# A planner's exp costs, the first block's PSUM halves, and when the last block's Q is made, in a fused attention and MLP block

## The chip, the cores and the metric

One core of a Trainium2 chip runs the kernel. The metric is device time in microseconds (us) of one execution. Before the change it is 780.84 us (median of 3 runs, 779.88 to 781.1). The engines are PE (TensorE: matmuls), DVE (VectorE), ACT (ScalarE), POOL (GpSimd) and SP (SyncE, which issues nearly all DMAs). Each works through its own queue in order and waits on semaphores for the others.

## The reference

One transformer block on 2048 tokens of 512 features, with 32 heads of 16 columns. Shift, scale and gate of both halves come from a conditioning row `c`.

```python
mod = (silu(c) @ w_mod)               # sa, ca, ga, sb, cb, gb: six rows of 512
h = layernorm(x) * (1 + ca) + sa
q, k, v = split_heads(h @ wqkv)       # 32 heads x 16
p = softmax(q @ k.T * 16 ** -0.5)
x = x + ga * ((p @ v) @ wo)
h = layernorm(x) * (1 + cb) + sb
x = x + gb * (gelu(h @ w1 + b1) @ w2 + b2)     # 512 -> 1376 -> 512
```

## The kernel before

**Blocks and runs.** The tokens are cut into four blocks of 512; a partition holds four tokens of a block (t = 0 to 3). For each block the kernel norms and transposes the tokens, projects K, V and Q, and then goes through its *runs*. A run is one block of queries against all 2048 keys for four heads, which lie side by side in the four row groups of 32 partitions. One key tile (128 keys) of a run gives four *scores*, matrices of 128 by 512, one a head. The first three blocks have 24 runs (block, group of 128 columns `cc`, parity of the head). The last block is cut differently: a run takes half of the queries for both parities (runs 24 to 29), and its last 256 queries go in quarters of 128 (runs 30 to 33; `tile_of` says which tokens: t = 2 for runs 30 and 31, t = 3 for 32 and 33). In all there are 2048 scores; run 24 begins at score 1536.

**Two ways to exponentiate.** Most scores are computed by PE into one of two PSUM tensors, `st3` (three banks) and `st2` (two), in turn, and exponentiated by ACT in one instruction of three or two scores (`qk_a`, L1022). The rest go one at a time into an `ax` bank, where DVE makes 16-bit integers `ph` of them whose bits are read as bf16 (L1063); four more integer additions on the whole tile (L1079 on DVE for three of them, and for the fourth either pieces on POOL, L1101, or what is left on DVE, L1095) and five sets of scaled values `VX` average the error of that approximation. `next_tile` gives key tiles to ACT or to DVE as either runs dry. Weighted sums of V, and of ones for the denominators, gather in the bank `od` (`pv_op`, L1162).

**Normalising.** When a run ends, `normalise` copies `od` (L1201), sends the denominators through DRAM to spread them over partitions (DMAs L1207, L1209, reciprocal on DVE L1212, DMAs L1217 and four of L1222), multiplies on POOL (L1228) and shifts rows into place (four DMAs, L1189). For the last runs `quick` does it on DVE alone: transpose, reciprocal, transpose, multiply (L1450 to L1456).

**The order.** Nothing above runs in the order it is written. `Plan` is a list scheduler in Python: every operation has an engine, a cost in us, the operations it depends on, and a priority; the planner starts what can start first, breaks near ties by priority plus a pseudo-random `spread` (one entry of `SEEDS` for each 12.5 us), and emits the instructions in that order. `A_US` is its cost of an exp of one, two or three scores. `later` holds back PE work that is not due yet: it starts only when PE has been less than full lately (`fill_at`). A `chain` is a group of matmuls into one `ax` bank, cut into pieces that the planner may put other work between. There are two `ax` banks.

**Q.** `want_q(g)` asks for the query projections up to group g. For the last block, groups 12 to 15 serve runs 24 to 27 first (and 28 to 33 again). A Q is four matmuls (L833), one DVE copy (`qs`, L869) and eight DMAs of 16 rows on SP's queue (`qm<-qs`, L875). `qk_deps` asks when the scores of a run are made; `due` tells when the matmuls stop being held back.

**The first norm.** `first_norm` is the way to the first exp: DVE makes statistics (L681, L682), POOL the power -1/2 (L692), DVE the normed tokens z (L698), PE the modulation columns (L675, from four loads of `w_mod`) and the transposes (L811), and DVE and ACT apply the modulation (L706, L703). *Part* 0 is tokens t = 0 and 1, part 1 is t = 2 and 3; j = 0 to 3 are the four column groups of 128. In the kernel before, DVE's j (0 and 1) lie in one PSUM tensor and ACT's (2 and 3) in the other, both parts of it in different banks. In the built program the transposes of part 1 into a tensor wait for the engine that reads part 0 out of it.

Of the kernel before, what the change touches and what calls it, by code (L numbers as in the profile page):

```python
# [12 lines left out]
ALU = mybir.AluOpType  # L13
# [50 lines left out]
SEEDS = (105, 215, 995, 503, 989, 957, 458, 92, 83, 614, 508, 48, 986, 458, 1, 279, 770, 174, 798, 975, 118, 230, 617, 767, 151, 936, 102, 752, 533, 869, 305, 310, 674, 762, 539, 481, 234, 244, 942, 69, 6, 273, 821, 447, 288, 502, 920, 725, 621, 485, 469, 573, 221, 692, 877, 666, 310, 622, 566, 733, 603, 368, 946, 826)  # L64
# [222 lines left out]
def kernel(  # L287
# [37 lines left out]
    COLD, EARLY = 4.4, 4.6  # L325
    SPAN = (3, 2)
    POOL_US, POOL_MIN = 0.68, 0.5
    A_US = {1: 0.49, 2: 0.9165, 3: 1.3435}
# [50 lines left out]
    def prog():  # L379
        return units[0] / 2  # L380
# [37 lines left out]
    def later(o):  # L418
        return o.kind not in ("qkA", "qkD", "pv", "last", "part", "heat") and o.kind not in urgent and o.due > prog()
# [135 lines left out]
    for h in range(2):  # L555
        o_x0 += 2 * [dma(lambda o, h=h: nc.sync.dma_start(out=o_x[0].tile[:, 2 * h:2 * h + 2, :],
                                                         in_=x_src[0][:, 2 * h:2 * h + 2, :]),
                         (o_x[0],), kb=210, prio=0.2 * h - 5.0)]
# [10 lines left out]
    def load_mod(j):  # L569
        def go(o):  # L570
            first[j] = nc.sync.dma_start(out=mod_cols(j), in_=wm_src[:, j, 0:2 * D])
        return dma(go, (o_mod,), kb=250, prio=0.2 * j - 4.6)
# [205 lines left out]
    def first_norm(kind):  # L778
# [10 lines left out]
        def scale(t):  # L789
# [5 lines left out]
              for t in range(TPB)]  # L795
# [3 lines left out]
                0.17, [mm] + o_plus, lat=0.03, prio=0.0, rel=(mm,))  # L799
# [3 lines left out]
        for part in range(2):  # L803
            for half, e in enumerate(("DVE", "ACT")):
                def view(half=half, part=part):
                    return banks[half].tile.bitcast(BF16)[:, 2 * part * QB:2 * part * QB + QB]

                def tr(o, half=half, part=part, view=view):
                    for j in range(2):
                        for t in range(2):  # L810
                            nc.tensor.transpose(out=view()[:, (2 * j + t) * P:(2 * j + t + 1) * P],  # L811
                                                in_=z.tile[:, 2 * part + t, (2 * half + j) * P:(2 * half + j + 1) * P],
                                                identity=ident)
                trs.append(op("PE", tr, 4 * 0.0575, za[2 * part:2 * part + 2] + [banks[half], o_id], lat=PEL,
                              mode=("full", 0), kind=kind, rel=(z,), prio=0.0))
                for n in range(2):
                    j = 2 * half + n
# [892 lines left out]
```

## Time and profile before

| | us |
|---|---|
| median of 3 runs (range) | 780.84 (779.88 to 781.1) |
| the profiled execution | 780.36 |
| its span (first to last instruction) | 778.5 |
| begin to first exp on ACT | 14.56 |
| first exp to end of the last | 745.2 |
| behind the last exp | 18.7 |

The span is what the profile covers; 1.86 us of the profiled execution lie around it. The granted TensorE clock is full throughout. The page of the profile gives each engine's busy time and the costliest groups of instructions; a row of the timeline is start, length, engine, line, operation and tile, and in brackets the idle time of the engine before it and what ended that.

### The profile page before, as it was taken

The page shows a single profiled execution, that of the slowest core. Times are in us where ns is not written, and L with a number is a line of the kernel's source. Part 1 is how long each engine was busy: PE and PEld are TensorE (multiplying, and loading weights), DVE is VectorE, ACT ScalarE, POOL GpSimd, SP SyncE. Part 2 cuts the span into 40 slices and gives each one's busy share as a digit, 9 for nine tenths or more (in the row PEclk, how much of TensorE's full clock was granted, in tenths as well). Part 3 has the DMA queues.
Part 4 walks back from the last instruction along what each step waited for, and adds up shares of the span by engine and source line. Part 5 has one row for each costly group of instructions (what it writes and reads, how often), then busy time and mean ns, then how long its engine had stood idle before and what let it go on. Part 6 is the DMA issues. An engine that isn't in the chain of part 4 may idle for free.

```text
span 778.5 us, 22044 instructions
## 1 busy us (share of the span) xinstructions
PE 726.3 (93%) x8886; PEld 274.8 (35%) x8964; DVE 725.6 (93%) x1294; ACT 751.3 (97%) x671; POOL 242.1 (31%) x466
## 2 busy tenths in 40 slices
PE   8899989999999999999999999999989999999998
PEld 3433333233332232232322232222334443444565
DVE  6889979999999999999999999998989999989984
ACT  4999999999999999999999999999989999999995
POOL 6522433512454532233324123322121222410310
PEclk9999999999999999999999999999999999999999
DMA  7152001100021101000100000001110001001000
GB/s 217 38 164 64 19 16 43 27 23 12 11 77 22 29 18 51 17 23 10 39 19 23 29 17 19 24 18 32 30 56 22 18 19 37 26 16 32 27 6 29
DMA packets 35248, 27.65 MB, mean 36 GB/s; under 512 B 18029, under 2 KB 29010, under 8 KB 35146
## 3 DMA queue, kind: packets, MB, share of 16 engines
q1 hardware_dynamic: 35138, 26.24, 12.1%
q8 instruction: 70, 1.15, 0.7%
q14 instruction: 32, 0.26, 0.1%
q10 hardware_dynamic: 8, 0.00, 0.0%
HBM read 20.64 MB, written 2.60 MB: 30 GB/s over the span
## 4 chain that ended last, share of the span: by engine, by line
ACT 36%; PE 27%; DVE 22%; issue 11%; DMA 2%; POOL 1%; SPq 0%; DVEq 0%; POOLq 0%; ACTq 0%
ACT pt L1022 35%; DVE ph L1063 10%; PE od L1162 8%; PE st L974 7%; DVE sh L1079 6%; PE ax L1335 3%; PE ax L974 2%; PE ax L1400 2%; DVE ln_s L681 2%; PE ax L833 1%; DMA dc<-dn 1%; DVE sh L1095 1%; DVE OD L1201 1%; PE ax L1329 1%; ACT g L1417 1%
## 5 line engine op out<-in xcount | busy, mean ns | idle before, releaser
L1022 ACT ACTIVATE pt<-st 128x1536 bf16<-128x1536 f32 x626 | 711.6, 1317 | 6.9 <-PE ax L974 3.7
L1063 DVE TENSOR_SCALAR ph<-ax 128x512 int16<-128x512 f32 x484 | 317.2, 683 | 20.0 <-PE ax L974 18.0
L974 PE MATMUL st<-qm,kT 32*128 32x512 bf16 (+1 forms) x1664 | 246.1, 370 | 21.0 <-ACT pt L1022 15.7
L1079 DVE TENSOR_SCALAR sh<-ph 128x2048 int16<-128x2048 int16 x363 | 242.5, 699 | 2.0 <-PE od L1162 1.2
L1101 POOL TENSOR_TENSOR sh<-ph,pair_sh 128x256 int32<-128x256 int32 x198 | 119.4, 611 | 286.5 <-DVE sh L1079 184.6
L974 PE MATMUL ax<-qm,kT 32*128 32x512 bf16 (+1 forms) x512 | 169.8, 367 | 9.5 <-DVE ph L1063 5.8
L1162 PE MATMUL od<-sh,VX 128*32 128x512 bf16 (+2 forms) x2640 | 171.5, 327 | 2.7 <-DVE sh L1079 2.0
L974 PEld LDWEIGHTS <-kT 32*128 32x128 bf16 x2176 | 81.1, 91 | 237.6 <-issue 225.1
L1162 PE MATMUL od<-pt,VEB 128*32 128x512 bf16 (+2 forms) x2156 | 141.6, 324 | 0.8 <-ACT pt L1022 0.3
L1162 PEld LDWEIGHTS <-VX 128*32 128x32 bf16 x2640 | 61.1, 95 | 84.0 <-issue 73.2
L1162 PEld LDWEIGHTS <-VEB 128*32 128x32 bf16 x2816 | 65.4, 96 | 70.3 <-issue 56.1
L1095 DVE TENSOR_SCALAR sh<-ph 128x2048 int16<-128x2048 int16 (+3 forms) x95 | 52.8, 563 | 0.3
L1228 POOL TENSOR_TENSOR OT<-OD,RB 128x256 bf16<-128x256 f32 x37 | 27.2, 745 | 75.2 <-DVE sh L1079 58.1
L1162 PE MATMUL od<-ph,VEB 128*32 128x512 bf16 (+2 forms) x660 | 48.2, 326 | 0.7 <-DVE OD L1201 0.7
L1400 PE MATMUL ax<-blk,W 128*128 128x512 bf16 (+1 forms) x153 | 40.5, 352 | 1.3 <-issue 0.6
L901 POOL TENSOR_SCALAR VX<-VEB 128x128 bf16<-128x128 bf16 x64 | 25.2, 394 | 38.7 <-DVE VEB L713 35.5
L1335 PE MATMUL ax<-w,g 128*128 128x512 bf16 x110 | 30.9, 381 | 1.8 <-DVE ph L1063 1.1
L833 PE MATMUL ax<-blk,w 128*128 128x512 bf16 x92 | 29.9, 382 | 2.0 <-issue 0.9
L1228 POOL TENSOR_TENSOR OS<-OD,RB 128x256 bf16<-128x256 f32 x24 | 17.3, 728 | 42.0 <-DVE sh L1079 23.6
L1407 DVE TENSOR_SCALAR g<-ax,b1c 128x512 bf16<-128x512 f32 x33 | 24.5, 744 | 0.2
L1335 PEld LDWEIGHTS <-g 128*128 128x128 bf16 x187 | 15.4, 97 | 23.1 <-issue 11.9
L681 DVE BATCH_NORM_STATS2 ln_s<-xb 128x6 f32<-128x512 bf16 x31 | 21.1, 680 | 1.4 <-DMA xb<-in_A_x_dram 1.4
(125 smaller groups left out, 408.3 us busy)
## 6 DMA issues: line engine op xcount, KB each, us to landing
RB<-rn SPq DMA_DIRECT2D x120, 64.0 KB
xb<-in_A_x_dram SPq DMA_DIRECT2D x7, 512.0 KB
qm<-qs SPq DMA_DIRECT2D x120, 16.0 KB
out_dram<-o SPq DMA_DIRECT2D x15, 128.0 KB
W<-in_B_w_dram SPq DMA_DIRECT2D x1, 1376.0 KB
w<-in_A_wqkv_dram SPq DMA_DIRECT2D x3, 384.0 KB
g<-in_w_mod_dram SPq DMA_DIRECT2D x4, 256.0 KB
xb<-in_w_mod_dram SPq DMA_DIRECT2D x2, 512.0 KB
```

What stands on the lines that cost most here:

```text
L681: nc.vector.bn_stats(out=st6, in_=src)
L833: return chain([(lambda ps, j=j: nc.tensor.matmul(out=ps[:, 0:QB], lhsT=w.tile[:, j, cc * P:(cc + 1) * P], rhs=o_h[b].tile[:, j, :], start ...
L974: nc.tensor.matmul(out=o.tile[:, k * QB + n * w:k * QB + (n + 1) * w], lhsT=kT[cc][kb][rows, ko * P:(ko + 1) * P], rhs=qm.tile[rows, par, ...
L1022: nc.scalar.activation(out=e.tile[:, 0:len(got) * QB], in_=o.tile[:, 0:len(got) * QB], func=ACT.Exp, scale=ESC)
L1063: nc.vector.tensor_scalar(out=ph.tile[:, o.row * QB:(o.row + 1) * QB], in0=o.tile, scalar1=PH_B, scalar2=0.0, op0=ALU.add, op1=ALU.max)
L1079: sh = op("DVE", lambda o, j=j: nc.vector.tensor_scalar(out=o.tile, in0=first.tile, scalar1=PH_SH[j], scalar2=None, op0=ALU.add), 0.6, es, ...
L1095: return nc.vector.tensor_scalar(out=sh.tile[:, at], in0=first.tile[:, at], scalar1=PH_SH[-1], scalar2=None, op0=ALU.add)
L1101: return nc.gpsimd.tensor_tensor(out=sh.tile[:, at].bitcast(I32), in0=first.tile[:, at].bitcast(I32), in1=pair_sh[:, 0:1].to_broadcast([P, ...
L1162: nc.tensor.matmul(out=o_od[r].tile[32 * i:32 * i + 32, to:to + w], lhsT=v_tile(k, ph)[:, c0:c0 + 32], rhs=got[i][:, n * w:(n + 1) * w], s ...
L1228: two = beside(lambda c: nc.gpsimd.tensor_tensor(out=both_heads(OT.tile, tile_of[r]) if r in tile_of else OT.tile[:, c], in0=OD.tile[:, c] ...
L1335: nc.tensor.matmul(out=ps, lhsT=g[:, f, col:col + P], rhs=rhs[:, c], start=(f == 0), stop=(f == NF - 1))
L1400: mm = chain([(lambda ps, f=f, j=j, f0=f0: nc.tensor.matmul(out=ps[:, (f - f0) * N:(f - f0 + 1) * N], lhsT=W1[:, j, f * P:(f + 1) * P], rh ...
```

## The change

- **Costs of exps**: `A_US` is 0.012 us smaller for one score and 0.011 for two and three; `COLD` and two costs of loads (`kb`) and of the first modulation change too, all in the planner's accounts alone. All 64 `SEEDS` are new (not shown).
- **Pieces of a chain that has begun** are not held back by `later` any more.
- **The first norm**: the two PSUM tensors now hold part 0 and part 1, each with all four j in one bank, so DVE and ACT both read both; PE transposes a part in one operation of eight. The modulation columns get a lower priority than the z of the last tokens.
- **Q of the last block**: group r - 8 is asked for by run r, and its due time is one run earlier for groups 13 to 15.
- **Run 30** is normalised by `quick` too, and POOL's multiplications of the last six runs are not held back until DVE leaves room.

```diff
-    COLD, EARLY = 4.4, 4.6
+    COLD, EARLY = 4.6, 4.6
-    A_US = {1: 0.49, 2: 0.9165, 3: 1.3435}
+    A_US = {1: 0.478, 2: 0.9055, 3: 1.3325}
...
     def later(o):
-        return o.kind not in ("qkA", "qkD", "pv", "last", "part", "heat") and o.kind not in urgent and o.due > prog()
+        return not o.cont and o.kind not in ("qkA", "qkD", "pv", "last", "part", "heat") and o.kind not in urgent and o.due > prog()
...
-                         (o_x[0],), kb=210, prio=0.2 * h - 5.0)]
+                         (o_x[0],), kb=210 if h else 315, prio=0.2 * h - 5.0)]
...
-        return dma(go, (o_mod,), kb=250, prio=0.2 * j - 4.6)
+        return dma(go, (o_mod,), kb=200 if j else 450, prio=0.2 * j - 4.6)
...
         mA = op("DVE", lambda o: nc.vector.tensor_tensor(out=modA, in0=mm.tile[:, 0:2 * NC], in1=plus, op=ALU.add),
-                0.17, [mm] + o_plus, lat=0.03, prio=0.0, rel=(mm,))
+                0.17, [mm] + o_plus, lat=0.03, prio=0.51, rel=(mm,))
...
         for part in range(2):
-            for half, e in enumerate(("DVE", "ACT")):
-                def view(half=half, part=part):
-                    return banks[half].tile.bitcast(BF16)[:, 2 * part * QB:2 * part * QB + QB]
...
+            def view(j, part=part):
+                return banks[part].tile.bitcast(BF16)[:, j * HB:(j + 1) * HB]
+
+            def tr(o, part=part, view=view):
+                for j in range(NC):
+                    for t in range(2):
+                        nc.tensor.transpose(out=view(j)[:, t * P:(t + 1) * P],
+                                            in_=z.tile[:, 2 * part + t, j * P:(j + 1) * P], identity=ident)
+            trs.append(op("PE", tr, 8 * 0.0575, za[2 * part:2 * part + 2] + [banks[part], o_id], lat=PEL,
+                          mode=("full", 0), kind=kind, rel=(z,), prio=0.0))
+            for j in range(NC):
+                e = ("DVE", "ACT")[j // 2]
+                done[j].append(op(e, lambda o, j=j, e=e, part=part, view=view: modulate(
+                    e, h.tile[:, j, part * HB:(part + 1) * HB], view(j), modA, j),
+                    0.32 if e == "DVE" else 0.46, (trs[-1], mA, h), prio=0.3 if part else 0.55, rel=(banks[part],)))
...
     def qk_deps(r, kts):
-        want_q(r // 2 + 2 if r < LAST * 8 else r - LAST * 4 + 3)
+        want_q(max(r // 2 + 2, r - LAST * NC + NC))
...
     def normalise(r):
-        if r == NR - 2:
+        if r in (NR - 4, NR - 2):
+            if r == NR - 4:
+                o_OT[runs[r]] = op("NIL", None, 0.0, (), lat=0.0, prio=0.0, acq=r_OT)
+                o_OT[runs[r]].two = []
             OT = o_OT[runs[r]]
-            OT.two = OT.two + [dma(lambda o: shift(OT, OT, 3), [quick(r, OT)], kb=32, n=4, prio=0.0)]
+            OT.two = OT.two + [dma(lambda o: shift(OT, OT, tile_of[r]), [quick(r, OT)], kb=32, n=4, prio=0.0)]
...
-            out=both_heads(OT.tile, tile_of[r]) if r in tile_of else OT.tile[:, c], in0=OD.tile[:, c], in1=o5.tile[:, c], op=ALU.mult), (OT,), (OD, o5), n=w // HB)
+            out=both_heads(OT.tile, tile_of[r]) if r in tile_of else OT.tile[:, c], in0=OD.tile[:, c], in1=o5.tile[:, c], op=ALU.mult), (OT,), (OD, o5), n=w // HB, soon=r >= NR - 6)
...
-    def beside(fn, deps, rel=(), prio=0.5, n=2):
+    def beside(fn, deps, rel=(), prio=0.5, n=2, soon=False):
...
-                   prio=prio, kind="beside", rel=rel, port=True, gate=lambda: plan.beside(POOL_MIN))
+                   prio=prio, kind="beside", rel=rel, port=True, gate=None if soon else lambda: plan.beside(POOL_MIN))
...
-            due(32 + APR * (first_run(q_made[0]) - 1) - 48)
+            due(32 + APR * (first_run(q_made[0]) - (1 if b < LAST or cc == 0 else 2)) - 48)
```

More of the change, by code (lines that the diff above doesn't have):

```diff
@@ L63 @@
 SPREAD = 0.15
-SEEDS = (105, 215, 995, 503, 989, 957, 458, 92, 83, 614, 508, 48, 986, 458, 1, 279, 770, 174, 798, 975, 118, 230, 617, 767, 151, 936, 102, 752, 533, 869, 305, 310, 674, 762, 539, 481, 234, 244, 942, 69, 6, 273, 821, 447, 288, 502, 920, 725, 621, 485, 469, 573, 221, 692, 877, 666, 310, 622, 566, 733, 603, 368, 946, 826)
+SEEDS = (623, 394, 452, 481, 475, 192, 433, 445, 275, 443, 224, 731, 768, 647, 975, 271, 840, 404, 636, 74, 28, 160, 309, 953, 860, 509, 279, 931, 560, 488, 582, 267, 702, 277, 253, 477, 729, 467, 373, 534, 867, 269, 472, 929, 60, 252, 569, 867, 547, 163, 471, 295, 975, 958, 772, 370, 541, 402, 517, 137, 699, 251, 764, 993)
 HEAT = 1.5
@@ L803, in first_norm @@
         for part in range(2):
-            for half, e in enumerate(("DVE", "ACT")):
-                def view(half=half, part=part):
-                    return banks[half].tile.bitcast(BF16)[:, 2 * part * QB:2 * part * QB + QB]
[L808 to L817, printed above, removed]
-                    done[j].append(op(e, lambda o, j=j, n=n, e=e, part=part, view=view: modulate(
-                        e, h.tile[:, j, part * HB:(part + 1) * HB], view()[:, n * HB:(n + 1) * HB], modA, j),
-                        0.3 if e == "DVE" else 0.39, (trs[-1], mA, h), prio=0.3 if part else 0.55, rel=(banks[half],)))
+            def view(j, part=part):
[12 more added lines that the diff above has]
+                    0.32 if e == "DVE" else 0.46, (trs[-1], mA, h), prio=0.3 if part else 0.55, rel=(banks[part],)))
         return h, [op("NIL", None, 0.0, x, lat=0.0, prio=0.0) for x in done], za, trs, mA
```

## The prediction

> **What bounds the kernel now.** I read the busy times by engine first, then the same in three stages cut at the first exp and behind the last one, then ACT's instructions by form. The columns of the second fence are length of the stage and busy us of PE, weight loads, DVE, ACT and POOL, with instruction counts, then clock, DMA share and GB/s.
>
> ```profile
> PE 726.3 (93%) x8886; PEld 274.8 (35%) x8964; DVE 725.6 (93%) x1294; ACT 751.3 (97%) x671; POOL 242.1 (31%) x466
> ```
>
> ```profile
> 0.00:14.56 14.56, 11.88 (x80) 5.28 (x82) 8.31 (x25) 4.07 (x8) 9.67 (x52) 1.00 0.77 233
> 14.56:759.78 745.22, 699.32 (x8669) 259.92 (x8744) 709.10 (x1252) 738.12 (x645) 231.92 (x414) 1.00 0.12 32
> 759.78:778.50 18.72, 15.10 (x153) 9.61 (x143) 8.23 (x18) 9.12 (x19) 0.55 (x1) 0.99 0.09 30
> ```
>
> ```profile
> L1022 ACT ACTIVATE pt<-st 128x1536 bf16<-128x1536 f32 x313 | 478.7, 1529 | 2.9 <-PE st L974 1.5 <-PE ax L974 0.9
> L1022 ACT ACTIVATE pt<-st 128x1024 bf16<-128x1024 f32 x312 | 345.2, 1106 | 4.0 <-PE ax L974 2.8 <-PE st L974 0.8
> ```
>
> The middle stage is ACT's. Exps overlap, so their rows' lengths (1529 and 1106 ns) are not what one costs; the starts of successive exps in the trace are 1.330 us apart behind one of three scores and 0.903 behind one of two when nothing is late. 313 x 1.330 + 312 x 0.903 + 0.48 for the one single is 698.5. ACT's other work there (GELUs and table loads 22.3, K copies 2.6, modulations 3.0) is 27.9. So 745.2 - 698.5 - 27.9 = 18.8 us are waits, 2.5%. DVE, counted by its own spacing of starts, stands 4% to 9% still in most windows of 100 us, and only 1.5% from 300 to 400, so the two are nearly balanced there. The end stage is a closed chain on PE (last fence).
>
> **The change, part by part.** Where I give counts of the changed program, they are from the order of its instructions, which the build shows; all durations are rows or start spacings of the trace above.
>
> *Moved work.* ACT gets four scores more (314 exps of three, 313 of two, no single): 1.330 + 0.903 - 0.48 = **+1.75 us** on the bounding engine. DVE loses 4 `ph` (4 x 0.60), 3 shifts (3 x 0.60) and, since POOL takes 215 pieces instead of 198, ten rests (seven of four at 0.60 and eight of one at 0.20 fewer, five of three at 0.47 more: 3.5); `quick` once more instead of a copy and a reciprocal adds 1.0. Together 6.7 us less on DVE. It is not on the path by itself, since DVE waits for PE more often than ACT for DVE. POOL's 17 pieces (17 x 0.61 = 10.4 us) lie in its 69% of idle time; without that cover DVE would do them at 0.13 each, 2.3 us.
>
> *Waits of ACT.* 18.8 us, of which Q (next part) is 2.3. The rest comes where PE has too much other work between two groups of scores. I counted that work in the order of both programs: 0.216 us for 512 columns (the spacing of full matmuls), a quarter of it for each of four weighted sums and a third for each score, which run side by side, and 0.1 for each change between these kinds. Of the stretches between two groups, 38 hold over 0.4 us more than the exp before them lasts; such stretches had a wait of 0.13 us on average in the trace, the rest 0.02. In the changed order there are 24, and the classes below that hardly move: 14 x 0.13 = **-1.8 us**. That is the effect that new costs, seeds and unpaced chains have on PE's order; chains that are not paced add no instruction. The bounds are far apart. The old accounts charge 313 x 0.0135 + 312 x 0.0135 = 8.4 us more for the exps than the trace has, the new ones 627 x 0.0025 = 1.6. If the surplus was what ACT waited for, 6.8 us of waits go; if it was slack that hid late scores, 6.8 us come. I take -1.8, which is counted, and keep both ends.
>
> *Q of the last block.* The columns are start, length, engine, line and tile.
>
> ```profile
> 579.22 1.77 SPq L875 DMA_DIRECT2D qm<-qs  x3
> ...
> 581.70 0.37 PE L974 MATMUL ax<-qm,kT 32*128 32x512 bf16 x1 [2.14 <-DMA qm<-qs]
> ...
> 582.11 0.69 DVE L1063 TENSOR_SCALAR ph<-ax 128x512 int16<-128x512 f32 x1 [1.82 <-PE ax L974]
> ...
> 583.48 1.02 ACT L1022 ACTIVATE pt<-st 128x1024 bf16<-128x1024 f32 x1 [2.28 <-PE ax L974]
> ```
>
> The eight DMAs of run 25's Q stand in SP's queue between those of a softmax (`dn`, `dc`, `rn`); DVE's share of run 25 asks for it, PE stands, and ACT behind it for 2.28 us. Old order: PE makes this Q after 1557 scores, 43 ahead of the run; the next two after 1575 and 1595. New order: after 1462, 1539 and 1603, so run 25's is 95 scores (some 35 us at 745/2048 us a score) earlier, and the two others each come 125 scores ahead of their runs. **-2.3 us**; bounds -2.4 (all of it) and -1 (DVE's 1.82 us less work waiting there and another wait behind it). The first two of these Qs now give SP 16 DMAs in a row, some 0.63 us each, 10 us; behind them stand a store and a softmax's first DMA. `od` is copied to one of two buffers by then and a run lasts 745/32 = 23 us, so this hides; without that cover up to 10 us of one normalising would show.
>
> *The first norm.* Old order, from the trace:
>
> ```profile
> 9.34 0.94 PE L811 MATMUL st<-ident,z 128*128 128x128 bf16 x8
> 9.52 0.17 DVE L798 TENSOR_TENSOR modA<-ax,plus 128x8 f32<-128x8 f32 x1 [1.01 <-PE ax L675]
> 9.60 0.40 DVE L698 TENSOR_SCALAR z<-xb,mv,rs 128x512 bf16<-128x512 bf16 x1
> ...
> 10.86 1.05 DVE L706 TENSOR_SCALAR blk<-st,modA 128x256 bf16<-128x256 bf16 x3 [0.48 <-PE st L811]
> 11.39 0.38 PE L811 MATMUL st<-ident,z 128*128 128x128 bf16 x4 [0.57 <-ACT blk L703]
> ...
> 11.81 1.02 ACT L703 ACTIVATE blk<-st,modA 128x256 bf16<-128x256 bf16 x2 [0.47 <-PE st L811]
> ```
>
> What the change removes is the wait of 0.57 for ACT before the last four transposes; the last z also comes before `modA`, into DVE's idle 1.01. What it adds is seen in the built order alone: DVE and ACT now read one tensor, and each modulation but the first of a part waits for the other engine's. They take turns: DVE, ACT, DVE, ACT in part 0, and the same in part 1. With DVE 0.41, ACT 0.56, 0.06 between engines, and a start at 10.0 (PE's eight transposes ended at 10.28; three idle-filling matmuls of 0.44 fewer stand before them, of which the load of `w_mod` lets some 0.3 count): DVE 10.0, ACT 10.47, DVE 11.09, DVE on part 1 11.41, ACT on part 0 11.56, ACT on part 1 12.02, DVE 12.64, ACT 13.11 to 13.67. Before, ACT's last ended at 12.83. So the first exp is 0.84 us **later**, not earlier; bounds -0.9 (as if the engines ran side by side from 10.0) and +1.1. Part of it hides: DVE then reaches the modulation of block 1 with one pair of statistics less ahead of it (0.86 + 0.1), and ACT stood still 0.78 + 0.56 us around there at 24 to 25. ACT's own shift, 0.84 less half of that wait, leaves **+0.3**. The Trainium skill, "PSUM — Partial Sum Buffer", section "PSUM bank collisions raise a hardware error", says that two engines may not touch one bank in the same partitions at once, two reads included, and that such pairs have to be kept apart by semaphores. By that rule no other order was to be had once both engines' columns share a bank; no run here shows a collision. Moved loads (block 2's tokens one place up on SP, block 3's behind two of Q's DMAs, two weight loads down by one) hide: block 2 lands at 16.1 and is first read at 21.2.
>
> *The end.*
>
> ```profile
> 758.91 1.28 PE od L1162 x80
> 760.19 1.11 PE ax L1500 x18
> ...
> 762.17 0.93 PE ax L1335 x4
> 763.09 0.43 PE t L1462 x2
> 763.53 3.24 PE ax L1335 x15
> ...
> 773.31 1.69 PE ax L1335 x7
> ```
>
> This is the chain of waits: PE from the last weighted sums to the last output without a hole. Behind the last sums the new order leaves 11 matmuls of L1500 instead of 18: 7 x 0.062 = 0.43. The GELU that the matmuls of L1335 wait for hangs on ACT, which gives 0.13 back: **-0.3** (0 to -0.45). Run 30's `quick` spares seven DMAs and a POOL step, which nobody on the chain waits for.
>
> Sum: +1.75 - 1.8 - 2.3 + 0.3 - 0.3 = -2.35. The profiled execution took 780.36 (span 778.5 and 1.86 around it), 0.48 below the median; 780.36 - 2.35 = 778.0, and against the median 780.84 - 2.35 = **778.5**.
>
> **Rivals.** *The pace follows the accounts*: ACT's waits fall by 6.8 instead of 1.8, 778.5 - 5.0 = 773.5. For it: ACT is 97.5% full in the middle stage, so what spaces PE's scores spaces the kernel; DVE loses 6.7 us too. Against it: waits are many small ones (some 65 over 0.06 us), not an even widening; the usual spacing is already 1.330.
> *Slack gone* (the slower side): with the surplus goes what let ACT run ahead of late scores, and 6.8 us of waits come instead of 1.8 going: 778.5 + 8.6 = 787. It decides from 2.35 + 1.6 = 4 us of new waits. For it: ACT's floor rises by 1.75 whatever else happens, and no engine has 10% left. Against it: PE's long stretches fall from 38 to 24.
> *Turns do not bind*: if the modulations overlapped after all, the first exp would come 0.9 earlier and 778.5 - 1.2 = 777.3; the built order's waits speak against it.
> *The new Q does not arrive in time either* (the change does not do what it says): SP is full of softmaxes at the other runs too, and the 2.3 us stay: 780.8. Leads of 125 to 138 scores against 43 speak against it.
>
> **How the numbers follow.** Forecast 778.5 with its neighbours from 776 to 780.5: 0.54; the pace 0.2; slack gone 0.12; turns do not bind 0.06; Q late 0.08. A measurement of this kernel can tell about 0.2% (1.6 us) from no change. Faster by more than that (below 779.3): 0.62 (pace, turns, and two thirds of the forecast); within it (to 782.4): 0.23; slower: 0.15 (slack gone and the forecast's upper tail). The range reaches to the pace rival and half of the way to the slack one: 773.5 to 782.5.
>
> **What would show it.** In the profile after: 627 exps with waits near 15 us in the middle stage; no hole of 2 us near run 25 and `qm<-qs` well ahead of L974; first exp at 15.2 to 15.5 with ACT and DVE alternating in the modulation; the last stage 18.4. Waits over 20 us, or any DMA wait of more than 2 us that is new, make the prediction wrong.

## The result, and the profile after

| | before | after |
|---|---|---|
| median of 20 runs each on one chip (range), us | 779.72 (778.3 to 782.35) | 783.71 (778.7 to 789.6) |
| ratio to before, 95% interval | | 1.0042 (1.0025 to 1.0058) |
| profiled execution, us | 780.36 | 781.98 |
| its span | 778.51 | 780.21 |
| begin to first exp | 14.56 | 14.28 |
| first exp to end of the last | 745.20 | 747.33 |
| behind the last exp | 18.75 | 18.60 |

The change made the kernel slower by 0.4%, where 778.5 (773.5 to 782.5) was forecast. In the comparisons below an execution is left out where the clock was below full throughout (one of 12 of the kernel `gate_bare` ran at 0.752 from end to end and took 843.57 us).

The page's busy times after the change, then the three stages (length; busy us of PE, weight loads, DVE, ACT, POOL with instruction counts; clock, DMA share, GB/s), then ACT's exps by form:

```profile
PE 734.9 (94%) x8948; PEld 276.8 (35%) x8948; DVE 721.8 (93%) x1279; ACT 752.6 (96%) x672; POOL 251.9 (32%) x482
```

```profile
0.00:14.28 14.28, 11.49 (x81) 4.92 (x82) 8.35 (x25) 4.18 (x8) 10.50 (x54) 1.00 0.80 244
14.28:761.61 747.33, 708.35 (x8733) 262.76 (x8733) 705.04 (x1238) 739.27 (x645) 240.88 (x428) 1.00 0.11 31
761.61:780.21 18.60, 15.02 (x136) 9.12 (x134) 8.41 (x18) 9.13 (x20) 0.55 (x1) 1.00 0.09 29
```

```profile
L1020 ACT ACTIVATE pt<-st 128x1536 bf16<-128x1536 f32 x314 | 485.9, 1548 | 5.1 <-PE st L972 2.4 <-PE od L1160 1.5 <-PE ax L972 0.5
L1020 ACT ACTIVATE pt<-st 128x1024 bf16<-128x1024 f32 x313 | 351.1, 1122 | 3.4 <-PE ax L972 1.7 <-PE st L972 1.5
```

The two profiled executions differ by 1.6 us, less than the medians, and all of it is in the middle stage. By the starts of exps as before, 314 x 1.330 + 313 x 0.903 = 700.3, and ACT's other work there is 28.1, so 747.33 - 700.3 - 28.1 = 19.0 us are waits (before, by the same count, 18.6, of which 2.4 were the late Q of run 25; its row shows 2.28 of idle time). PE's busy times, 726.3 and 734.9, can't be compared: the profile before holds 443 records of full matmuls of 512 columns where this one has 517, and a second profile of the changed kernel (`after_again`) lacks 74 too and shows 730.0. What slowed PE down shows in the same view in steps of 3.4 us (the clock is the third number from the end):

```profile
115.00:118.40 3.40, 3.22 (x47) 1.16 (x39) 3.40 (x7) 3.40 (x4) 1.42 (x2) 1.00 0.00 0
118.40:121.80 3.40, 2.60 (x28) 1.06 (x31) 3.37 (x10) 3.40 (x4) 1.97 (x3) 1.00 0.03 5
121.80:125.20 3.40, 3.40 (x31) 0.94 (x23) 2.60 (x5) 2.44 (x3) 1.35 (x3) 0.50 0.04 7
125.20:128.60 3.40, 3.24 (x43) 1.12 (x40) 1.89 (x5) 3.38 (x4) 0.86 (x2) 1.00 0.31 80
```

From 121.80 to 125.20 the granted clock is 0.50, ACT is busy for 2.44 of 3.40 us, and DVE stays short for one step more. The timeline of PE and ACT around it (start, length, engine, line, operation, tile, count, idle time before and what ended it):

```profile
117.32 0.39 PE L1160 MATMUL od<-pt,VEB 128*32 128x512 bf16 x4
...
118.01 0.35 PE L652 MATMUL ax<-sc,g 128*128 128x1 bf16 x8
118.23 0.32 PE L655 MATMUL ax<-warm 128*128 128x384 bf16 x1
...
119.57 0.35 PE L652 MATMUL ax<-sc,g 128*128 128x1 bf16 x8
119.79 0.32 PE L655 MATMUL ax<-warm 128*128 128x384 bf16 x1
...
120.73 0.25 PE L652 MATMUL ax<-sc,g 128*128 128x1 bf16 x4
...
121.61 0.92 PE L1160 MATMUL od<-pt,VEB 128*32 128x512 bf16 x8
...
122.31 0.65 PE L1160 MATMUL od<-ph,VEB 128*32 128x512 bf16 x4
122.73 0.65 PE L1160 MATMUL od<-sh,VX 128*32 128x512 bf16 x4
...
124.46 2.49 ACT L1020 ACTIVATE pt<-st 128x1024 bf16<-128x1024 f32 x2 [0.95 <-PE ax L972]
```

The matmuls of L652 make the modulation of the attention's output, one column at a time: 128 rows by 128 columns of weights, and a single column streamed. It is a chain (`gate` in what follows), and its pieces stood between scores 272 and 298 before; not held back any more, they lie between 266 and 285, from 118.01 on with no weighted sum between them until 121.61. The clock falls just behind, four sums of L1160 take 0.65 us instead of 0.39, and ACT waits 0.95. The same profile has a second such stretch at 19.4 us; the profile before has none up to the last exp (one begins at 778.06, in its last 0.45 us).

### The profile page after: what moved, and what is told of

It reads as the page before. It is cut to its first block, busy times and chain, and to the rows that moved or that the text cites. A ratio compares the mean times of both kernels' runs of the same rounds, so it can differ in the third digit from the quotient of the medians.

```text
span 780.2 us, 22083 instructions
## 1 busy us (share of the span) xinstructions
PE 734.9 (94%) x8948; PEld 276.8 (35%) x8948; DVE 721.8 (93%) x1279; ACT 752.6 (96%) x672; POOL 251.9 (32%) x482
## 3 DMA queue, kind: packets, MB, share of 16 engines
q8 instruction: 70, 1.15, 0.6%
## 4 chain that ended last, share of the span: by engine, by line
PE 38%; ACT 29%; DVE 19%; issue 9%; DMA 3%; POOL 1%; SPq 1%; DVEq 0%; ACTq 0%
ACT pt L1020 26%; PE od L1160 14%; PE st L972 11%; DVE ph L1061 8%; DVE sh L1077 6%; PE ax L1336 4%; PE ax L1401 3%; PE ax L972 2%; PE ax L831 2%; ACT g L1418 1%; DMA w<-in_A_wqkv_dram 1%; DVE sh L1093 1%; DVE ln_s L681 1%; DVE g L1408 1%; DMA dc<-dn 1%
## 5 line engine op out<-in xcount | busy, mean ns | idle before, releaser
L1077 DVE TENSOR_SCALAR sh<-ph 128x2048 int16<-128x2048 int16 x360 | 239.9, 696 | 1.8 <-PE od L1160 1.0
L1099 POOL TENSOR_TENSOR sh<-ph,pair_sh 128x256 int32<-128x256 int32 x215 | 130.6, 616 | 276.6 <-DVE sh L1077 183.7
L1160 PE MATMUL od<-sh,VX 128*32 128x512 bf16 (+2 forms) x2624 | 167.7, 326 | 4.1 <-DVE sh L1077 3.0
L972 PEld LDWEIGHTS <-kT 32*128 32x128 bf16 x2176 | 84.0, 91 | 239.8 <-issue 227.4
L972 PE MATMUL ax<-qm,kT 32*128 32x512 bf16 (+1 forms) x508 | 164.2, 368 | 3.9 <-DVE ph L1061 2.6
L1160 PE MATMUL od<-pt,VEB 128*32 128x512 bf16 (+2 forms) x2160 | 143.5, 326 | 0.0
L1160 PEld LDWEIGHTS <-VEB 128*32 128x32 bf16 x2816 | 65.3, 96 | 74.7 <-issue 58.9
L1160 PEld LDWEIGHTS <-VX 128*32 128x32 bf16 x2624 | 60.0, 95 | 79.8 <-issue 69.0
L1093 DVE TENSOR_SCALAR sh<-ph 128x2048 int16<-128x2048 int16 (+3 forms) x85 | 49.5, 588 | 1.2 <-PE od L1160 1.2
L1160 PE MATMUL od<-ph,VEB 128*32 128x512 bf16 (+2 forms) x656 | 48.4, 327 | 1.6 <-DVE OD L1202 1.1
L1401 PE MATMUL ax<-blk,W 128*128 128x512 bf16 (+1 forms) x176 | 43.8, 355 | 0.6 <-DVE ph L1061 0.3
L831 PE MATMUL ax<-blk,w 128*128 128x512 bf16 x120 | 35.3, 383 | 2.2 <-DVE blk L706 1.3
```

The source lines that it names most:

```text
L831: return chain([(lambda ps, j=j: nc.tensor.matmul(out=ps[:, 0:QB], lhsT=w.tile[:, j, cc * P:(cc + 1) * P], rhs=o_h[b].tile[:, j, :], start ...
L972: nc.tensor.matmul(out=o.tile[:, k * QB + n * w:k * QB + (n + 1) * w], lhsT=kT[cc][kb][rows, ko * P:(ko + 1) * P], rhs=qm.tile[rows, par, ...
L1077: sh = op("DVE", lambda o, j=j: nc.vector.tensor_scalar(out=o.tile, in0=first.tile, scalar1=PH_SH[j], scalar2=None, op0=ALU.add), 0.6, es, ...
L1093: return nc.vector.tensor_scalar(out=sh.tile[:, at], in0=first.tile[:, at], scalar1=PH_SH[-1], scalar2=None, op0=ALU.add)
L1099: return nc.gpsimd.tensor_tensor(out=sh.tile[:, at].bitcast(I32), in0=first.tile[:, at].bitcast(I32), in1=pair_sh[:, 0:1].to_broadcast([P, ...
L1160: nc.tensor.matmul(out=o_od[r].tile[32 * i:32 * i + 32, to:to + w], lhsT=v_tile(k, ph)[:, c0:c0 + 32], rhs=got[i][:, n * w:(n + 1) * w], s ...
```

## The experiments

"Clock" is the mean of the granted clock over a kernel's runs, and time at half clock is (1 - clock) x 2 x span. Kernels that stand in one group by their number under "before" were measured together, on one chip, against the same runs of the kernel before; the five groups stand on four chips. Begun chains, seeds and costs all act on the planner, so a kernel is either *planned anew* (all its order can move) or keeps the order, as said.

| kernel | median us (n) | before us | ratio (95%) | clock |
|---|---|---|---|---|
| before_again | 780.24 (10) | 779.6 | 1.0006 (0.9996 to 1.0015) | 0.9955 |
| after_again | 784.60 (10) | 779.6 | 1.0046 (1.0025 to 1.0067) | 0.9944 |
| gate_warm | 779.44 (12) | 779.6 | 0.9998 (0.9985 to 1.0011) | 0.9987 |
| zeros_thin | 787.49 (6) | 779.6 | 1.0099 (1.0078 to 1.0120) | 0.997 |
| paced | 790.42 (5) | 779.96 | 1.0150 (1.0126 to 1.0173) | 0.9954 |
| gate_paced | 785.48 (6) | 779.96 | 1.0075 (1.0058 to 1.0093) | 0.9953 |
| before_unpaced | 793.90 (4) | 779.96 | 1.0182 (1.0169 to 1.0195) | 0.9905 |
| q_only | 779.10 (12) | 779.96 | 0.9989 (0.9980 to 0.9997) | 0.9980 |
| gate_bare | 782.49 (11) | 780.58 | 1.0024 (1.0011 to 1.0037) | 0.993 |
| before_bare | 781.20 (12) | 780.58 | 1.0012 (1.0000 to 1.0024) | 0.9953 |
| sums_first | 780.91 (12) | 780.58 | 1.0013 (0.9997 to 1.0028) | 0.9986 |
| old_seeds | 784.28 (6) | 780.58 | 1.0048 (1.0030 to 1.0065) | 0.9965 |
| fill0_again | 782.97 (11) | 780.49 | 1.0028 (1.0016 to 1.0041) | 0.9932 |
| fill4_again | 783.58 (12) | 780.49 | 1.0043 (1.0022 to 1.0064) | 0.9931 |
| fill8 | 784.32 (9) | 780.49 | 1.0043 (1.0027 to 1.0058) | 0.9943 |
| fill12_again | 779.70 (12) | 780.49 | 1.0006 (0.9990 to 1.0022) | 0.9983 |
| late_dc | 781.02 (12) | 779.73 | 1.0021 (1.0006 to 1.0037) | 0.9952 |
| warm_late | 778.53 (12) | 779.73 | 0.9987 (0.9974 to 1.0000) | 0.9985 |

### Both kernels again, and array work added

`before_again` and `after_again` are the two kernels unchanged.

> The kernel before, unchanged, for its clock. Theory C (the loss is TensorE at half clock: in the 20 runs of the changed kernel time rises by 0.77 us for each us at half clock, from 778.7 with none to 789.6 with 27): this kernel's runs lie mostly at a mean clock of 0.997 to 1.0 (none or one or two stretches of 3.4 us at half clock) and near 779.7. Theory P (the new order itself waits more, whatever the clock): the clock here spreads as widely as in the changed kernel, 0.983 to 1.0, and the time does not follow it.

> The changed kernel, unchanged, for a second place of its half-clock stretches. Theory C: mean clock 0.990 to 0.998, time 780 to 786 along 779 + 0.77 us for each us at half clock; stretches of 3.4 us at half clock again begin behind windows in which PE has little array work, above all at 117 to 126 us where the matmuls of one column for the second modulation (L652) now run together. Theory P: waits of ACT of over 1 us stand at other places than the half-clock stretches.

The loss came again, and a kernel's time goes with its time at half clock. (The 0.77 us of both expectations is for each us of (1 - clock) x span, which is 0.38 for each us at half clock as defined above.) Theory C missed the clock of `before_again`, 0.9955 and not 0.997 to 1.0: the kernel before has time at half clock as well, and it costs less there. Over 42 executions of the changed kernel (the 20 of the result, `after_again`, `fill4_again`) a straight line is 779.7 + 0.39 us for each us at half clock (correlation 0.90; mean 9.9 us at half clock), so 1.3 us for one stretch of 3.41 us; over 129 executions of the kernel before it is 779.2 + 0.20 (correlation 0.66; mean 5.0 us). 9.9 x 0.39 - 5.0 x 0.20 = 2.9 us of the loss go with the clock, and 0.5 us do not. A line through executions doesn't tell cause from companion (a late transfer can cost time and halve the clock as well); the kernels below change the work itself.

`gate_warm` has 12 fillers of L655 in the chain of modulation columns instead of 4; the rest of the order is the same:

```diff
-        if m % 2 and warmer:
+        for _ in range(1 + m % 2 if warmer else 0):
```

> The changed kernel with 8 more filler matmuls of 384 columns (1.3 us of array work) among the matmuls of one column at 118 to 126 us; every other instruction stands in the same order. Theory C: the stretch at half clock behind 118 to 122 us is gone, one stretch of 3.4 us less on average, mean clock up by about 0.002 to 0.004 and time down by 1.0 to 2.6 us against the changed kernel (783.7 to about 781.5 to 782.5). Theory P: no gain, or 0.3 us more for PE's extra work.

It took the whole loss back, although PE has 8 x 0.16 = 1.3 us more to do. That is more than theory C gave for one stretch (1.0 to 2.6 us). `zeros_thin` adds 66 sets of four zero matmuls wherever the planner's account had little array work in 3.4 us:

```diff
-            if o.extra:
+            if o.extra or left[r] > 0 and plan.thin():
```

> The changed kernel with 66 more sets of four matmuls that add zeros to the running sum, wherever the array work that the scheduler counts for the last 3.4 us is under 2.0 us; every other instruction stands in the same order, and PE has 14 us more work in all, spread over the run. Theory C: the clock stays at 0.998 to 1.0, the runs close up, and the time comes down to 778 to 780.5. Theory P: the time stays at 783 to 785 or rises by some of the 14 us.

Its profile had the stretches at 19.1 and 121.5 us all the same, since the sums to which the zeros are tied don't reach these places (the first sum of the profile after starts at 20.47 us, and none runs from 118.01 to 121.61), and its waits rose to 24.8 us. Some 14 us of zeros cost 2.9 us more than the changed kernel on the same chip. In the place of `gate_warm` a filler paid, spread over the middle stage it did not.

### Pacing: all orders planned anew

`paced` lets `later` hold back begun chains again, `gate_paced` only the modulation's chain; `before_unpaced` is the kernel before with the one edit.

```diff
-        return not o.cont and o.kind not in (
+        return o.kind not in (
```

> The changed kernel with begun chains paced again, as before the change; everything else of the change stays, and the order is planned anew. In it the one-column modulation matmuls spread over 31 scores again (the 273rd to the 304th; before 272 to 298, changed 266 to 285), and no stretch is longer than 14 scores without weighted sums (changed 18, before 16). Theory C (half clock behind the bunched modulation columns): no stretch at half clock between 116 and 128 us, mean clock over the runs at least 0.997 against 0.9936, and 778 to 780.5 us. Theory W (weighted sums pushed back by begun chain pieces): the wait near 705 us of 1.7 goes, waits of ACT in the middle stage 16 to 19 us; with C 777 to 779.5. Rival S (the new seeds and costs give a worse order whatever is paced): 782 to 786, and the clock tells nothing.

> The changed kernel in which only the chain of the modulation (one-column matmuls) is paced again; all other begun chains stay unpaced. The chain spreads over 22 scores (273 to 295), the longest stretch without weighted sums is 15. Theory C: no half clock at 116 to 128 us, mean clock at least 0.996, 778.5 to 780.5. Theory W: ACT's waits in the middle stage like the changed kernel's without its dips, 18 to 20, so 779 to 780.5 and slower than the kernel with all chains paced. Rival S: 782 to 786.

> The kernel before, with the one edit that begun chains are not paced; planned anew. Its modulation columns lie between scores 274 and 292. Theory C, if unpaced chains alone are the cause: half clock of 3.4 us or more between 116 and 128 us in the profile or in most runs (mean clock 0.992 to 0.996), 781.5 to 785. Rival P (the unpaced pieces matter only together with the other edits, which move the modulation to another place): mean clock 0.997 as before, 778.5 to 781.

`paced` and `before_unpaced` missed every expectation, mine included; `gate_paced` came out where the rival S had it. Their longest waits lie elsewhere (`paced` at 298 to 304 and 557 to 564 us, `before_unpaced` at 367 to 371 and 596 to 608), `paced` also gives ACT 8.9 us more of exps (318 of three scores and 317 of two), `gate_paced` still had half clock at 122.2 us with the chain spread over 22 scores, and its end stage had 158 matmuls behind the last sum instead of 120 and took 22.16 us. So pacing can't be judged alone: with a rule altered, the 64 numbers of `SEEDS` give another order. `old_seeds` asks that directly: the changed kernel with the old numbers.

> The changed kernel with the 64 numbers by which the planner breaks near ties (SEEDS) of the kernel before; planned anew. Theory S (the numbers were fitted to one set of rules, and any other set of rules gets a random order): 783 to 794, as the three replanned kernels gave (785.5, 790.4, 793.9), with ACT's waits between 18 and 31. Rival R (the changed rules are better for themselves, and the numbers matter little): 778 to 782.

784.3, at the near end of what the theory of fitted numbers gave (783 to 794), though with waits of 16.6 us, fewer than it said. With the three above, orders planned with numbers that were chosen under other rules took 4 to 14 us more than the kernel before, more than any edit here brings. That the numbers had been fitted is argued from this, not shown.

### Q alone

```diff
-        want_q(r // 2 + 2 if r < LAST * 8 else r - LAST * 4 + 3)
+        want_q(max(r // 2 + 2, r - LAST * NC + NC))
```

(and the due time of the diff; the order is that of the kernel before up to about score 1532)

> The kernel before, with the two edits alone that make Q of the last block one run earlier; the order is that of the kernel before up to about score 1532. Theory Q (my term of -2.3): no wait of ACT over 0.5 us between 575 and 585 us, 777 to 778.2, ratio 0.997. Rival: the wait of 2.3 is given back later (the softmax behind the Q transfers late, or another wait of ACT over 1 us behind 580 us): 779 to 780.5.

The wait at run 25 is gone: ACT's exps run on from 568.92 for 22.03 us. But the ratio gives 0.9 us (0.2 to 1.6), not 2.3. 0.91 us comes back as a new wait that ends at 723.19 us, and 0.7 in the end stage, which has 26 matmuls of L1500 behind the last sum instead of 18 and takes 19.44 us. Both theories were half right.

### Sums ahead of projections

In every profile of the changed order ACT waits about 1.5 us near 708 (1.54 in the row below; 1.7 by the spacing of starts, counted from the exp that starts at 705.8); no profile of the kernel before has this wait. The changed kernel's timeline, weighted sums and projections on PE and ACT's wait:

```profile
700.37 0.39 PE L1160 MATMUL od<-pt,VEB 128*32 128x256 bf16 x8
701.02 0.61 PE L1336 MATMUL ax<-w,g 128*128 128x512 bf16 x2
701.88 1.25 PE L1336 MATMUL ax<-w,g 128*128 128x512 bf16 x5
...
706.61 0.84 PE L1160 MATMUL od<-sh,VX 128*32 128x256 bf16 x24
707.92 1.06 PE L1160 MATMUL od<-pt,VEB 128*32 128x256 bf16 x32
708.42 1.45 ACT L1020 ACTIVATE pt<-st 128x1536 bf16<-128x1536 f32 x1 [1.54 <-PE od L1160]
```

PE makes projections from 701 to 706 and no sum, the four buffers `pt` of each kind of exp fill up, and ACT stands. `sums_first` is `gate_warm` with the sums first for 5 us of the plan:

```diff
-            return 0.5 + same
+            return (1.1 if 690 < plan.now < 695 else 0.5) + same
```

> The kernel with 12 fillers (779.4) in which, for 5 us of the plan at about 700 us, the last blocks' projection pieces stand behind the weighted sums instead of ahead of them, so that the longest stretch without a sum falls from 18 scores to 12; behind the last sum there are then 33 matmuls of L1501 more. Theory W (the order costs this wait by itself): the wait of 1.7 at 705.8 falls below 0.7 and 1 us is gained, 778 to 779. Theory B (PE has no time left there, and what the wait loses is work that has to be done before the end anyway): the wait falls, the last stage grows by 33 x 0.06 = 2 us to 20.6, and the time is 779.5 to 781.

Its stages:

```profile
14.19:754.83 740.64, 694.02 (x8654) 260.16 (x8729) 704.13 (x1234) 736.97 (x644) 244.75 (x434) 1.00 0.11 32
754.83:778.42 23.59, 18.74 (x228) 12.38 (x218) 12.41 (x30) 9.12 (x19) 1.09 (x2) 0.99 0.07 24
```

The wait is gone and the middle stage 6.1 us shorter than in `gate_warm` (746.78, one stretch at half clock included). Of these 6.1, 1.8 are four scores that ACT has no longer in this order (313 exps of three, 312 of two, one single). But the end stage is 5.0 us longer, more than the 2 that theory B gave for it, and nothing is gained (ratio to before 1.0013 against 0.9998). That is theory B's time: near 700 us ACT waits for PE, and what PE is spared there it does before the end in any case.

### How much array work keeps the clock

Without the fillers, in both kernels:

```diff
-        if m % 2 and warmer:
+        if m % 2 and warmer and False:
```

> The changed kernel without the 4 idle-filling matmuls of 384 columns inside the chain of modulation columns (the run with 12 of them gave 779.4, the changed kernel with 4 gave 784.6); order otherwise the same, 4 x 0.16 us less work of PE. Theory C (too little array work around the one-column matmuls halves the clock): more windows below 1.25 us of array work from 114 to 126 us, mean clock over the runs below 0.992 with two or more stretches of 3.4 us there, 785 to 790. Rival N (the clock falls for another reason, or costs nothing, and the 12 fillers helped by shifting the order in time): 783 to 785 or less, mean clock 0.993 to 0.995.

> The kernel before without the same 4 fillers; order otherwise the same. Its modulation columns are spread over 26 scores instead of 19. Theory C in its full form (the bunching takes the place of fillers: where the columns are spread, the sums and scores between them keep the array busy enough): mean clock 0.994 or above, 779 to 781. If spread columns are as near the edge (before's poorest window there holds 1.23 us), half clock appears near 120 us in most runs, mean clock 0.990 to 0.994 and 781 to 784.

`gate_bare` was not slower than the changed kernel, as rival N had it and against my theory; `before_bare` lost 0.1% and had half clock at 126.7 us, so the spread columns before the change stood near the edge too. As `gate_warm` and `gate_bare` were on different chips, 0, 4, 8 and 12 fillers then ran on one:

> The changed kernel without fillers in the modulation chain, beside 4, 8 and 12 on the same chip. Theory C (array work in a window of 3.4 us decides): the lowest mean clock of the four, 0.991 to 0.994, and a stretch at half clock between 118 and 130 us in the profile. By 0.3 to 0.8 us for each us at half clock (the slopes seen between runs of one kernel), 781.5 to 786. Theory N (it has nothing to do with the fillers): all four between 781 and 785 with clocks within 0.002 of one another.

> The changed kernel unchanged (4 fillers). Theory C: mean clock between that of 0 and that of 8 fillers, about 0.994; 783 to 785, and a stretch at half clock between 118 and 126 us. If it is slower than the kernel without fillers by over 1 us again at the same clock, then the price of a stretch depends on the work that it falls on, not on its length alone. Theory N as above.

> The changed kernel with one filler for each modulation column group (8 instead of 4), order the same. Theory C: mean clock 0.995 to 0.998 and 780 to 783, between 4 and 12 fillers. Theory N: as the others.

> The changed kernel with 12 fillers. Theory C: the highest clock of the four, at least 0.997, no stretch at half clock between 114 and 130 us, 778.7 to 780.5, at least 2 us below the changed kernel of the same chip. Theory N: 781 to 785.

No graded dose in the time: 0, 4 and 8 lie within their intervals of one another (`fill8` missed theory C in time and clock), and 12 is 3 to 5 us faster at a clock of 0.998. With 12 (`fill12_again`), the same stretch of time as above reads:

```profile
115.00:118.40 3.40, 3.06 (x44) 1.31 (x41) 3.40 (x7) 3.40 (x4) 2.06 (x3) 1.00 0.00 0
118.40:121.80 3.40, 3.27 (x46) 1.33 (x42) 3.37 (x9) 3.40 (x4) 1.39 (x3) 1.00 0.03 5
121.80:125.20 3.40, 3.36 (x46) 1.23 (x39) 2.66 (x7) 3.40 (x4) 1.30 (x2) 1.00 0.05 10
```

The profile with 8 has no half clock there either, but at 280 and 349 us. What the 19 profiles (all but `gate_bare`'s) have in common was counted so: in each trace a grid of 3.413 us laid through its first drop; in each window from 13 to 760 us the *array work*, the sum over its matmuls of columns streamed x 0.2155/512 us, times the share of the array's rows and of its columns that the weights fill; windows already at half clock left out.

| array work in a window | windows | half clock in the next |
|---|---|---|
| below 1.15 us | 15 | 15 |
| 1.15 to 1.4 | 47 | 11 |
| 1.4 and above | 4038 | 2 |

Eight of these profiles lack some 74 records of full matmuls, so array work is a little too low in them; the other eleven alone give 9 of 9, 8 of 28 and 2 of 2332. Without the shares the same sum tells it far worse: 8 of the 28 drops follow windows with 4.5 us and more (scores and sums side by side count several times). So does PE's busy time: in the window before the drop at 121.80 PE was busy for 2.60 of 3.40 us, and some 560 of the windows without a drop behind them are no busier than the busiest of the 28 (3.00 us). The longest pause of PE inside any of the 28 windows is 1.81 us (`q_only`).

At the chain itself there is a dose. The poorest 3.41 us that can be laid anywhere over it hold 0.39 us of array work with no filler (`fill0_again`), 0.71 with 4 (in all five profiles with 4), 1.19 with 8 and 1.46 with 12 (in all four); in the kernel before they hold 1.25, without its fillers 0.92. In the profiles the clock fell there for 10.2 us with none, for 3.4 to 10.2 us in four of the five with 4, and in none with 8 or 12. The drops of one trace lie whole multiples of 3.413 us apart (30.00 between the two of the profile after), and where this grid falls differs between executions. So a thin place is caught in one execution and missed in another: in `late_dc`, below, the poorest 3.41 us hold 0.71 too, but the windows of its grid there (laid through its only drop, at 777.39 us) hold 1.25 and more, and its clock stayed full.

### A softmax that comes back late

The profile of `after_again`, DVE, PE and ACT near 348 us, and the transfers on SP before it:

```profile
341.84 0.53 SPq L1208 DMA_DIRECT2D dn<-OD  x1
342.47 1.77 SPq L873 DMA_DIRECT2D qm<-qs  x3
344.34 0.53 SPq L1210 DMA_DIRECT2D dc<-dn  x1
```

```profile
348.30 0.25 DVE L1213 RECIPROCAL dc<-dc 128x16 f32<-128x16 f32 x1 [2.00 <-DMA dc<-dn]
348.47 0.63 DVE L1077 TENSOR_SCALAR sh<-ph 128x2048 int16<-128x2048 int16 x1
...
349.15 0.40 PE L1160 MATMUL od<-sh,VX 128*32 128x512 bf16 x4 [1.77 <-DVE sh L1077]
...
349.97 1.02 ACT L1020 ACTIVATE pt<-st 128x1024 bf16<-128x1024 f32 x1 [1.30 <-PE st L972]
```

The reciprocal is put into DVE's queue where the planner expects its sums back; they land 3.96 us after the issue of `dc<-dn` here, 2.4 us in the first profile of the same kernel. Everything behind it on DVE waits, then the sums on PE, then ACT; the window from 346.9 holds 0.59 us of array work, and the clock halves at 350.3. In the seven profiles of the changed order (with 0 to 12 fillers) DVE waits 0.6 to 1.1 us so at 280 and, in six, 0.2 to 2.0 us at 345; half clock followed at 348 to 350 in the three with 0.99 us or more. In the four profiles that keep the order of the kernel before up to there, none waits near 345; two wait at 278 and 281 (0.52 and 0.89), and those of the kernel before itself at 698 and 721 (0.6 to 0.8). `late_dc` moves these two reciprocals one and two instructions down DVE's queue and nothing on the other engines; `warm_late` does so with 12 fillers.

```diff
-        o3 = op("DVE", lambda o: nc.vector.reciprocal(
+        o3 = op("DVE", lambda o: late.append([3 if r in (10, 13) else 0, lambda: nc.vector.reciprocal(
...
-            o.fn(o)
+            o.fn(o); o.eng == "DVE" and getattr(self, "tick", int)()
```

(`tick` counts down and emits what is due; the transfer behind the reciprocal emits it at the latest)

> The changed kernel (4 fillers) with two reciprocals of softmax sums moved down DVE's queue, that of the 11th run by one instruction (0.6 us) and that of the 14th by two (1.3 us); PE's, ACT's and SP's orders are the same. DVE's wait for them falls from 0.6 to 1.1 us and 0.2 to 2.0 us to below 0.5 and 0.8. Theory D (the late softmax is one of the things that set off stretches at half clock): none at 280 and 345 to 352 us in the profile, mean clock 0.995 to 0.996, 781.5 to 783.3, since those near 19 and 118 stay. Rival: the stretches all go back to the modulation columns, and the time stays at 783.5 to 784.6 with the clock at 0.993 to 0.994.

> The same two moves in the kernel with 12 fillers. Theory C with D: mean clock 0.999 or above, 778.5 to 779.6, at most 2 of 12 runs above 780.5 (4 of 12 without the moves), ratio to the kernel before 0.997 to 0.999. Rival: as without the moves, 779.4 to 779.8 and 0.9983 to 0.9987.

`late_dc` lost about half of what the changed kernel lost (ratio 1.0021 against 1.0042, 1.0046 and 1.0043), at the clock that theory D gave and a little below its time. The intervals overlap, and the chips differ; the 42 executions of the changed kernel together lie 0.28% above it (standard error 0.09%). Its profile shows no wait of DVE for a reciprocal, but it fell on the fastest of 12 executions, at full clock, so it can't tell which stretches the move prevents:

```profile
0.00:14.21 14.21, 11.41 (x81) 4.89 (x82) 8.34 (x25) 4.18 (x8) 10.52 (x54) 1.00 0.80 244
14.21:757.74 743.53, 704.98 (x8733) 262.44 (x8733) 704.58 (x1238) 738.54 (x645) 241.73 (x428) 1.00 0.12 32
757.74:776.33 18.59, 15.01 (x136) 9.12 (x134) 8.41 (x18) 9.14 (x19) 0.55 (x1) 1.00 0.09 29
```

743.53 - 700.3 - 28.2 = 15.0 us of waits, 778.12 us in all. `warm_late` is the fastest of all kernels, 778.53, 0.13% below the kernel before (interval 0.26% to 0), though its clock, 0.9985, is below theory D's 0.999: with both places mended the loss is gone, and a small gain is likely but not clear of noise.

## Why the prediction was wrong

**What bounds the kernel**: right that ACT sets the middle stage (its other work there is 28.1 us by the rows, not 27.9). Short in that PE's work was counted only where it makes ACT wait: `sums_first` shows that what PE is spared there it does at the end.

**Moved work, +1.75**: +1.8 came (700.3 against 698.5, by the spacings of starts, which did not change). DVE's relief was over-sized: 725.6 to 721.8, 3.8 us instead of 6.7.

**Waits, -1.8**: the step that failed. "I counted that work in the order of both programs ... In the changed order there are 24": the count takes a matmul's columns as its whole cost, at full clock. The 32 one-column matmuls count for almost nothing in it, so it can't see that bunched together they let the clock fall. The prediction had no term for the clock at all, though the window of the chain was in the built order to be seen. In place of 1.8 us less came more: without the late Q the kernel before has 18.6 - 2.4 = 16.2 us of waits, and the changed kernel has 19.0 in the first profile and 22.2 in `after_again`. By the spacing of starts, 1.14 and 1.31 of the 19.0 are waits behind the two stretches at half clock, and 1.71 is the wait near 708, which the new order makes and the count doesn't name. The waits of DVE for a DMA were left out likewise, which a count of PE's stretches can't show.

In the one profile of the changed order with neither half clock before the last exp nor a late softmax, `late_dc`'s, the waits are 15.0, and 14.7 (18.8 - 1.8 - 2.3) was forecast. That agreement is luck as far as the runs tell: it is another kernel, in its fastest execution. The changed kernel itself had four of its 42 executions at full clock (0.999 and above), 778.70 to 779.86 us, no lower than the kernel before at full clock (see the base, below). So the forecast gain is missing without half clock too.

**Q, -2.3**: the mechanism was right. The changed kernel's transfers and ACT at run 25:

```profile
542.09 10.54 SPq L873 DMA_DIRECT2D qm<-qs  x16
```

```profile
569.57 20.60 ACT L1020 ACTIVATE pt<-st 128x1536 bf16<-128x1536 f32 x18
```

The sixteen transfers in a row came as counted (10.54 us), and no exp waits near run 25. The lower bound, -1, was nearer to what it is worth: 0.9 in `q_only`, where another wait came behind it, as that bound had it.

**First norm, +0.3 (first exp 0.84 later)**: turns as said, the start not.

```profile
8.75 0.15 DVE L798 TENSOR_TENSOR modA<-ax,plus 128x8 f32<-128x8 f32 x1
9.02 0.41 DVE L706 TENSOR_SCALAR blk<-st,modA 128x256 bf16<-128x256 bf16 x1
9.47 0.56 ACT L703 ACTIVATE blk<-st,modA 128x256 bf16<-128x256 bf16 x1 [4.75 <-DVE blk L706]
10.06 0.73 DVE L706 TENSOR_SCALAR blk<-st,modA 128x256 bf16<-128x256 bf16 x2 [0.63 <-ACT blk L703]
10.51 1.02 ACT L703 ACTIVATE blk<-st,modA 128x256 bf16<-128x256 bf16 x2 [0.48 <-DVE blk L706]
11.56 0.41 DVE L706 TENSOR_SCALAR blk<-st,modA 128x256 bf16<-128x256 bf16 x1 [0.77 <-ACT blk L703]
12.01 0.56 ACT L703 ACTIVATE blk<-st,modA 128x256 bf16<-128x256 bf16 x1 [0.48 <-DVE blk L706]
```

The eight modulations alternate and take 9.02 to 12.57, 3.55 us instead of 2.86 (9.97 to 12.83) before. They began a whole us earlier than the 10.0 taken, because `modA` came at 8.75 instead of 9.52, and the first exp was 0.28 earlier. In eleven profiles that begin in the changed order it is at 14.14 to 14.37, in the four that begin in the order before at 13.06 to 15.28: against that scatter neither sign is settled.

**The end, -0.3**: -0.15, for 7 matmuls of L1501 fewer.

**The base**: the sum was made on an execution of 780.36. Executions of the kernel before at full clock (0.999 and above) had medians of 778.7 to 779.3 in the five groups, so that one stood 1.1 us and more above them; where it lost this isn't shown. At full clock `warm_late` has 778.4 against 779.1 on the same chip: with 12 fillers and the moved reciprocals the change is worth 0.7 us there, not 2.35.

**Rivals**: "Q late" (780.8) and "slack gone" (787) came nearest in time, 2.9 and 3.3 us off, and neither mechanism decided. The wait for Q is gone; and without the two waits behind half clock the profile after has 16.5 us of waits, where slack gone needs 6.8 more than the 16.2 of before. Of the two signs that were to make the prediction wrong the profile after shows none (19.0 us of waits, and DVE's waits for a softmax's DMA at most 0.79); `after_again` shows the first (22.2 us) and just not the second (2.00, where more than 2 was named). The range ended at 782.5; nothing in it stood for an execution that differs from the profiled one.

**Left open**: why one transfer of 8 KB takes 2.4 us in one execution and 4.0 in another; why 8 fillers, which lift the chain's poorest 3.41 us to 1.19, gave as much time at half clock over their executions as none, and 12 so much less; one profile a kernel doesn't tell where the stretches of the other executions lie, so how the loss divides between the chain, the late softmax and the first 20 us is open as well; and what each edit of the planner would bring with numbers chosen for it.

## What to carry to other kernels

Before a reordering is judged by how evenly an engine's work is spread, look at what the work is: matmuls that stream one column are short in time and leave the array nearly empty, and here, bunched together, they slowed what came behind them. When an order is planned by program, the built order's thin places (array work in each 3.4 us, and each instruction that heads a queue while its transfer is on the way) belong on the list beside the engines' sums. And the base of a small forecast should be several executions, with the clock of each, not the one that was profiled.

## What the runs showed of the hardware

The clock of TensorE halved for stretches of 3.41 us (or twice or three times that) without a pause of PE of that length, the longest being 1.81 us: fifteen of fifteen windows with under 1.15 us of array work in 3.41 us were followed by one, while PE's own busy share was 2.60 of 3.40 us in the case shown above. The Trainium skill, "TensorE: Matmul & The Clock Gate", section "HAM oscillation — how this bites in real kernels", gives the rule that PE must not idle for more than about 3.4 us; the length of the window agrees with the traces, but idle gaps are not what decided here. By the straight lines above, one such stretch cost an estimated 1.3 us in the changed kernel and 0.7 in the kernel before (0.39 and 0.20 us for each us at half clock).
